# A transformer block on one core: the first output projection's weights asked for together, divisions at 18 exponentials instead of 28, and block 0's statistics four exponentials later

## The chip, the core and the metric

The kernel runs on one core of a Trainium2 chip. The metric is the device time of one execution in microseconds (us). Engines are named as in the profile: PE (TensorE, matrix products), DVE (VectorE), ACT (ScalarE), POOL (GpSimd), SP (SyncE, which here issues the DMAs). Each engine works through its own instructions in the order in which they were written; semaphores tie the engines together.

## The reference

One transformer block with an adaptive layer norm, for 2048 rows of 512 features, 32 heads of 16, and a feed-forward layer of 1792. Everything is fp32.

```python
def _A_ref(x, wqkv, wo):                       # attention
    qkv = (x @ wqkv).reshape(B, S, 3, H, Dh).transpose(2, 0, 3, 1, 4)
    q, k, v = qkv[0], qkv[1], qkv[2]
    scores = einsum("bhqd,bhkd->bhqk", q, k) * Dh ** -0.5
    o = einsum("bhqk,bhkd->bhqd", softmax(scores), v)
    return o.transpose(0, 2, 1, 3).reshape(B, S, D) @ wo
def _B_ref(x, w1, b1, w2, b2):                 # feed-forward
    return einsum("bsf,fd->bsd", gelu(einsum("bsd,df->bsf", x, w1) + b1), w2) + b2
sa, ca, ga, sb, cb, gb = six rows of silu(c) @ w_mod
x = x + ga * _A_ref(layernorm(x) * (1 + ca) + sa, ...)
x = x + gb * _B_ref(layernorm(x) * (1 + cb) + sb, ...)
```

## The kernel before

**Tiles.** Where the result needs nearly full fp32, a value is kept as two pieces, a high and a low one, and a product is three matmuls (high × high, low × high, high × low). A weight tile that holds both pieces of 128 rows of `wo`, `w1` or `w2` has 512 KB. The rows are cut into four blocks of 512 queries.

**Stages.** A prologue, whose order is a list written out by hand, does the layer norm and the first projections. Then come 512 half-steps. They belong to 32 units (query block × group of four heads) of 16 half-steps each, and a half-step handles 128 keys. It has four score matmuls for the exponentials (L642, ACT's exponential at L649), four score matmuls ahead of that for the row maxima of a later unit (L390, DVE's reduction at L395), and the products of the probabilities with the values of an earlier half-step (`pv`, L676). Everything else of the block, that is the other projections, the output projection and the feed-forward layer, is background: groups of matmuls that add up in one bank named `bg`. A half-step takes six half-row matmuls of the current group along (L276). A half-step for which no group is ready is called empty here; it writes its fourth maximum's scores to the free `bg` bank, which is how the profile tells it apart. In the last 22 half-steps no maxima are left, and a half-step takes four half-row matmuls of background. What is still open after the 512th half-step is done in a tail without scores.

**What sets the order.** The Python program writes the instructions in the order in which they shall stand. Its clock `t` counts exponentials (in the tail every second matmul). `later(n, f)` writes the step `f` when n more exponentials have been written, and `soon(n, f)` does so too but also counts the step as owed until then. `work()` yields the background groups one after another and yields nothing where a condition isn't met; that makes a half-step empty. So a delay in the code is a place in the order, and what the engines do with it shows only in the trace.

**The steps that the change touches**, in the order in which they come:
- `proj_qk` (L300 and on): a projection group's end. ACT copies the bank (L310), POOL makes the two pieces (L311, L312), and a `soon` step stores them to memory (`store_qk`, L298 and L299, 768 KB in two DMAs on SP).
- `block0` waits until nothing is owed and no division is under way, then calls `open_ffn` (L684 and on), which gives up the pools of the projections and opens one pool for the output projection and the feed-forward layer in the same memory. A tile of the new pool waits for the last user of its memory.
- `wload` (L776 to L792) asks for the next weight tile in the order of use, at SP's line L791, if fewer than WB = 8 tiles are taken. Half-steps call it, at most once each.
- `o_prep` (L708 to L748), the softmax division for one quarter of a block's features: it asks for the denominators `dn` and the sums `ob`; then DVE's reciprocal (L724), a store of it (L728), a load spread over rows, `rb` (L734), and on POOL the product and its two pieces (L742 to L744). Each step comes a number of exponentials after the one before it: 14, 2, 5 and 7, which makes 28.
- `front(b)` (L812 and on), the output projection of a block: it waits for four divisions and four exponentials more, until all four `wo` tiles have been asked for, and then yields four groups of four half-steps each. Behind a group stand ACT's copy (L859), the addition of `x` on POOL (L862), and after a number of exponentials the statistics: two parts on DVE (L839), four exponentials apart, the aggregate and the factor (L842, L851, and L852 on POOL), then the normalization `xn` on POOL (L825). Block 0's last group takes a shorter way, on DVE.
- At a unit's end its maxima are brought together on DVE (L407, L409), split in two on POOL (L411, L412, tile `m`), stored (L416) and loaded into the rows of `qst` (L422). SP also asks for the keys (`kh`, L362), the values (`vg`, L595), `x` (L810), and stores the attention's sums (`ou`, L665).

Of the kernel before, what the change touches and what calls it, by code (L numbers as in the profile page):

```python
# [23 lines left out]
KC = D // P  # L24
NB = 4
# [45 lines left out]
def block_kernel(ctx: ExitStack, tc: tile.TileContext, x, wqkv, wo, w1, b1, w2, b2, c, w_mod, out):  # L71
# [4 lines left out]
    def pool(name, bufs=1, **kw):  # L76
        cm = tc.tile_pool(name=name, bufs=bufs, **kw)
        return cm, cm.__enter__()

    def close(*cms):  # L80
        for cm in cms:
            cm.__exit__(None, None, None)
# [78 lines left out]
    def stage(name):  # L161
        if first[0] and name in FIRST:
            return vpool.tile([P, D], F32, tag=name, name=name, bufs=FIRST[name])
        return spool.tile([P, D], F32, tag=name, name=name, bufs=STAGE[name])

    def pieces(name, dt=FR):
        return spool.tile([P, 2, D], dt, tag="parts", name=name, bufs=3)
# [83 lines left out]
    def later(n, f):  # L251
        if n:
            hooks.setdefault(clock["t"] + n, []).append(f)
        else:
            f()
# [3 lines left out]
    def soon(n, f):  # L259

        owed[0] += 1

        def g():
            owed[0] -= 1
            f()

        later(n, g)
# [27 lines left out]
    def store_qk(w, k, b, parts):  # L295
        stored.add((w, k, b))
        planes = qk_d[w][k].rearrange("i d o t -> (d o) i t")[:, :, b * TB : (b + 1) * TB]
        sy.dma_start(planes[:, 1 - w : 3 - w], parts.bitcast(F32))  # L298
        sy.dma_start(planes[:, 2 * w], parts[:, 0].bitcast(F32))  # L299

    def proj_terms(w, k, b):
        hi, lo = hT[b]
        t = wt_of[w, k]
        n = range(KC)
        return terms3([t[:, 0, i] for i in n], [t[:, 1, i] for i in n], [hi[:, i] for i in n], [lo[:, i] for i in n])

    def proj_qk(w, k, b):
        def evac(ps):
            parts, r = pieces("parts"), stage("pf")
            ac.activation(r, ps, AF.Copy)  # L310
            gp.tensor_copy(parts[:, 0], r)  # L311
            gp.tensor_tensor(parts[:, 1], r, parts[:, 0].bitcast(F32), op=ALU.subtract)  # L312
            soon(8, lambda: store_qk(w, k, b, parts))

        return proj_terms(w, k, b), "bg", evac

# [372 lines left out]
    def open_ffn():  # L689
        assert not preps and not owed[0]  # L690
        close(*pools["old"])
        pools["cm"], pools["f"] = pool("ffn", side="right")
        f = pools["f"]
        pools["x2"] = [[f.tile([P, D], F32, name=f"x2{n}{i}") for i in range(4)] for n in range(2)]

    pcs = []

# [6 lines left out]
    def tmp(name):  # L704
        if "f" in pools:
            return pools["f"].tile([P, D], F32, tag="t", name=name, bufs=8)
        return dvpool.tile([P, D], F32, tag="t", name=name, bufs=4)

    free_pc, busy, over = [0], [0], [False]

    def o_prep(b, k):

        dn = small.tile([P, 32], F32, tag="dn", name="dn")
        base = ou_d[b]
        sy.dma_start(dn, base[2 * k : 2 * k + 2].rearrange("g (j r) (a f) -> (g j) r a f", r=32, f=32)[:, DH])
        ob, rb = tmp("ob"), tmp("rb")
        for g in range(2):
            sy.dma_start(ob[g * 64 : (g + 1) * 64], base[2 * k + g].rearrange("(j r) t -> j r t", r=32)[:, :DH])
        eng = ve if over[0] else gp
        r = rden_d[b][k * 8 : (k + 1) * 8]  # L720
        busy[0] += 1

        def inv():
            ve.reciprocal(dn, dn)  # L724
            later(0 if over[0] else 2, store)

        def store():
            sy.dma_start(r.rearrange("h (a f) -> (h a) f", f=32), dn)  # L728
            later(1 if over[0] else 5, load)
            if over[0]:  # L730
                wload()

        def load():
            sy.dma_start(rb, bass.AP(tensor=r.tensor, offset=r.offset, ap=[[TB, 8], [0, DH], [1, TB]]))  # L734
            later(9 if over[0] else 7, div)
            if over[0]:
                for _ in range(6):
                    wload()
                load_x2(last, x2)

        def div():
            eng.tensor_tensor(ob, ob, rb, op=ALU.mult)  # L742
            eng.tensor_copy(pc(b, k, 0), ob)
            eng.tensor_tensor(pc(b, k, 1), ob, pc(b, k, 0).bitcast(F32), op=ALU.subtract)  # L744
            done[b] += 1
            busy[0] -= 1

        later(11 if over[0] else 14, inv)  # L748

    def try_prep():  # L750
        if not ready or not pcs:
# [26 lines left out]
    def wload():  # L778

        n = len(wt)  # L780
        if n == len(stream) or "f" not in pools:
            return
        key = stream[n]
        if extra:
            t = extra.pop()
        elif len(ringed) < WB or ringed[-WB] in used:
            t = pools["f"].tile([P, 2, D], FR, tag="w", name=f"w{key[1]}", bufs=WB)
            ringed.append(key)
        else:
            return  # L790
        sy.dma_start(t.bitcast(F32), {"o": wo_d, 1: w1_d, 2: w2_d}[key[1]][key[2]])  # L791
        wt[key] = t  # L792
# [14 lines left out]
    def load_x2(b, x2):  # L807
        for t in range(4):
            r0 = b * TB + t * P
            sy.dma_start(x2[t], x[r0 : r0 + P, :])  # L810

    def front(b, x2):  # L812


        later(9, lambda: load_x2(b, x2))
        yield from until(lambda: done[b] == KC - 1)
        yield from wait(4)
        yield from loaded(b, *[("o", k) for k in range(KC)])
        mv = small.tile([P, 4, 2], F32, tag="mv", name="mv")
        rs = {}  # L820
        xn = {}

        def norm(t):
            xn[t] = tmp("xn")
            (gp if b or t < 3 else ve).tensor_scalar(  # L825
                xn[t], x2[t], mv[:, t, 0:1], rs[t], op0=ALU.subtract, op1=ALU.mult)
            later(40, lambda: gp.tensor_tensor(x2[t], x2[t], b2_b, op=ALU.add))
            if b and len(xn) == 4:
                later(9, lambda: sides.extend([lambda fc=fc: trans(fc, "mx") for fc in range(KC)]))

        def stat(t):
            if b == 0 and t == 3:
                ln_stat(mv, t, x2[t])
                later(1, lambda: factor(t))
                return
            st = small.tile([P, 2, 6], F32, tag="bsh", name="bsh")

            def part(i):
                ve.bn_stats(st[:, i], x2[t][:, i * HD : (i + 1) * HD])  # L839

            def whole():
                ve.bn_aggr(mv[:, t], st)  # L842
                factor(t)

            part(0)
            later(4, lambda: part(1))
            later(8, whole)

        def factor(t):
            rs[t] = small.tile([P, 1], F32, tag=f"rt{t}", name=f"rt{t}")  # L850
            ve.tensor_scalar(rs[t], mv[:, t, 1:2], EPS, None, op0=ALU.add)  # L851
            gp.tensor_tensor(rs[t], rs[t], mhalf[:, 0:1], op=ALU.pow)  # L852
            later(3 if t < 3 else 2, lambda: norm(t))

        for t in range(4):

            def evac(ps, t=t):
                y = tmp("y")
                ac.activation(y, ps, AF.Copy)  # L859

                def add():
                    gp.tensor_tensor(x2[t], y, x2[t], op=ALU.add)  # L862
                    later(8 if b else 4 if t < 3 else 3, lambda: stat(t))

                later(2, add)

            yield o_terms(b, t, range(KC)), "bg", evac
        drop(b, *[("o", k) for k in range(KC)])
        t0 = clock["t"]

        def trans(fc, bk="bg"):
            ps = take(bk)
            for t in range(4):
                te.transpose(ps[:, t * P : (t + 1) * P], xn[t][:, fc * P : (fc + 1) * P], ident)  # L874
            h = tmp("h32")
            ac.activation(h, ps, AF.Identity, scale=modc[:, 1, fc, 0:1], bias=modc[:, 1, fc, 1:2])
            gp.tensor_copy(pc(b, fc, 0), h)
            gp.tensor_tensor(pc(b, fc, 1), h, pc(b, fc, 0).bitcast(F32), op=ALU.subtract)
            turned[fc] = clock["t"]

        turned = {}
        yield "ln"
        if b:
            yield from until(lambda: len(turned) == KC and clock["t"] >= turned[KC - 1] + 8)
            return
        yield from until(lambda: len(xn) == 4 and clock["t"] >= t0 + 9)
        for fc in range(KC):
            yield lambda fc=fc: trans(fc)
        yield from wait(4)
# [410 lines left out]
```

## Time and profile before

| | |
|---|---|
| median of 3 runs | 1693.07 us (1692.38 to 1693.36) |
| the profiled execution | 1691.76 us |
| its span, first to last instruction | 1690.0 us |
| granted TensorE clock, mean | 0.997 |
| background of the half-steps: `wo`, `w`×`g`, `pchi`×`w` matmuls | 192, 1056, 656 |
| half-step exponentials | 2048, 611 ns each |

The table of groups in the profile gives line, engine, operation, output tile and input tiles, shape and count, then the busy time and the mean time of one in ns. The timeline gives start, duration, engine, line, operation and, in brackets, the idle time just before and what ended it. `SPq` is the DMA queue of SP: the duration of its rows is the issue, not the transfer.

### The profile page before, as it was taken

Reading aid. Unit: us, or ns where it says so; the run is one execution under the profiler, and the core shown is the slowest. Engines: PE = TensorE matmul, PEld = TensorE weight load, DVE = VectorE, ACT = ScalarE, POOL = GpSimd, SP = SyncE. Lnnn points to the kernel's source line nnn. Section 1 sums busy time; section 2 is a strip of 40 time slices with the busy share of each in tenths; the row PEclk is TensorE's granted clock in tenths of the full one; section 3 lists DMA queues with packets and bytes.
Section 4 is the critical chain, followed back from the end, with each engine's and each line's share of the span. In section 5 each row is a group of like instructions: output and inputs, shape, how many; then the busy total and the mean of one; then the engine's idle time right before and its main releaser. Section 6 shows DMA issues by size and latency. Waiting matters only on the chain.

```text
span 1690.0 us, 32259 instructions
## 1 busy us (share of the span) xinstructions
PE 1670.4 (99%) x12121; PEld 919.3 (54%) x12121; DVE 1402.7 (83%) x2692; ACT 1238.0 (73%) x2379; POOL 692.0 (41%) x698
## 2 busy tenths in 40 slices
PE   7999999999999999999999999999999999999999
PEld 6655555555554455555555555555555555553777
DVE  8998888889889988898999888888999888880332
ACT  3358788788777788778877788778877788779131
POOL 7323443434211356405643447316633456226110
PEclk8999999999999999999999999999999999999999
DMA  9656666657557434326454454345453454333544
GB/s 297 204 175 189 219 208 208 219 185 229 145 152 220 118 90 119 90 47 175 118 161 106 114 164 121 84 117 140 115 164 79 131 145 107 84 96 109 208 153 157
DMA packets 137127, 251.88 MB, mean 149 GB/s; under 512 B 25854, under 2 KB 45324, under 8 KB 136972
## 3 DMA queue, kind: packets, MB, share of 16 engines
q1 hardware_dynamic: 135712, 248.19, 50.6%
q8 instruction: 96, 1.57, 0.4%
q10 hardware_dynamic: 1260, 1.63, 0.3%
q14 instruction: 59, 0.48, 0.1%
HBM read 188.49 MB, written 61.28 MB: 148 GB/s over the span
## 4 chain that ended last, share of the span: by engine, by line
PE 91%; DVE 4%; DMA 2%; ACT 2%; issue 0%; POOL 0%; SPq 0%; POOLq 0%; ACTq 0%; DVEq 0%
PE bg L276 40%; PE pv L676 29%; PE e L642 16%; PE mx L390 4%; DVE mxp L395 3%; ACT p L649 1%; DMA kh<-qk 1%; PE pr L276 1%; PE o L276 1%; PE warm L441 1%; PE mx L335 0%; DVE bst L237 0%; DMA qst<-qk 0%; PE mx L874 0%; DMA qk<-parts 0%; DMA wraw<-in_A_wqkv_dram 0%
## 5 line engine op out<-in xcount | busy, mean ns | idle before, releaser
L395 DVE TENSOR_REDUCE mxp<-mx 128x1 f32<-128x512 f32 x2034 | 1285.0, 682 | 143.3 <-PE mx L390 126.3
L649 ACT ACTIVATE p<-e 128x512 f32<-128x512 f32 x2048 | 1073.0, 611 | 272.5 <-PE mx L390 251.3
L390 PE MATMUL mx<-kh,qst 48*128 48x512 f32 x2034 | 835.6, 423 | 1.3 <-DVE mxp L395 1.0
L642 PE MATMUL e<-qst,kh 50*128 50x512 f32 x2048 | 777.9, 424 | 3.7 <-ACT p L649 3.6
L642 PEld LDWEIGHTS e<-qst,kh 50*128 50x128 f32 x2048 | 341.4, 185 | 429.6 <-ACT p L649 309.8
L676 PE MATMUL pv<-p,vg 128*32 128x512 f32 x4096 | 546.3, 605 | 0.3 <-ACT osb L663 0.3
L390 PEld LDWEIGHTS mx<-kh,qst 48*128 48x128 f32 x2034 | 367.0, 185 | 14.9 <-DVE mxp L395 9.7
L276 PE MATMUL bg<-w,g 64*128 64x512 f32 (+1 forms) x1056 | 264.3, 389 | 0.1
L276 PEld LDWEIGHTS bg<-w,g 64*128 64x128 f32 (+1 forms) x1056 | 196.0, 186 | 29.7 <-issue 0.5
L276 PE MATMUL bg<-pchi,w 64*128 64x512 f32 (+1 forms) x656 | 177.8, 391 | 0.0
L676 PEld LDWEIGHTS pv<-p,vg 128*32 128x32 f32 x4096 | 81.0, 108 | 171.7 <-issue 159.0
L276 PE MATMUL bg<-hThi,wqkv 64*128 64x512 f32 x560 | 153.1, 392 | 0.1
L276 PEld LDWEIGHTS bg<-pchi,w 64*128 64x128 f32 (+1 forms) x656 | 120.8, 185 | 25.6 <-DVE tick L1086 5.9
L276 PEld LDWEIGHTS bg<-hThi,wqkv 64*128 64x128 f32 x560 | 103.8, 185 | 14.1 <-DVE tick L1108 0.4
L918 POOL TENSOR_SCALAR s<-s 128x512 f32<-128x512 f32 x40 | 59.9, 1497 | 97.0 <-ACT s L916 96.6
L937 POOL TENSOR_TENSOR x<-y,x 128x512 f32<-128x512 f32 x28 | 36.0, 1285 | 153.0 <-ACT y L936 153.0
L276 PE MATMUL bg<-pclo,w 64*128 64x512 f32 (+1 forms) x328 | 88.5, 389 | 0.0
L276 PE MATMUL bg<-hTlo,wqkv 64*128 64x512 f32 x280 | 76.5, 392 | 0.0
L911 POOL TENSOR_TENSOR s<-h 128x512 f32<-128x512 f32 x40 | 41.7, 1042 | 69.2 <-ACT h L910 69.2
L276 PEld LDWEIGHTS bg<-pclo,w 64*128 64x128 f32 (+1 forms) x328 | 60.0, 184 | 13.1 <-DVE tick L1086 5.0
L276 PE MATMUL bg<-wo,pchi 64*128 64x512 f32 x192 | 59.3, 388 | 0.0
L411 POOL CAST m<-mt 128x32 fp32r<-128x32 f32 x32 | 6.8, 212 | 121.7 <-DVE mt L409 121.7
(165 smaller groups left out, 1373.8 us busy)
## 6 DMA issues: line engine op xcount, KB each, us to landing
kh<-qk SPq DMA_DIRECT2D x256, 192.0 KB
w<-w1s SPq DMA_DIRECT2D x56, 512.0 KB
w<-w2s SPq DMA_DIRECT2D x54, 512.0 KB
vg<-v SPq DMA_DIRECT2D x64, 332.0 KB
qk<-parts SPq DMA_DIRECT2D x32, 512.0 KB
qst<-qk SPq DMA_DIRECT2D x64, 192.0 KB
qk<-parts SPq DMA_DIRECT2D x32, 256.0 KB
ou<-osb SPq DMA_DIRECT2D x32, 256.0 KB
```

The costliest lines, as they stand in the source:

```text
L276: return te.matmul(ps, term[0][r], term[1][r], start=i == 0, stop=i == n - 1)
L390: te.matmul(ps, qst[u][r0 : r0 + KR, p, qc * P : (qc + 1) * P], kh(u, kr // 2)[r0 : r0 + KR, p, (kr % 2) * TB : (kr % 2 + 1) * TB], start= ...
L395: ins = ve.tensor_reduce(mxp[u][:, hc, kr : kr + 1], ps, axis=AX.X, op=ALU.max, negate=True)
L411: gp.tensor_copy(m2[:, 0], mt)
L441: te.matmul(warm[:, :P], ident, ident, start=True, stop=True)
L642: ins = te.matmul(ps, kh(u, kc // 8)[r0 : r0 + KX, p, (kc % 8) * P : (kc % 8 + 1) * P], qst[u][r0 : r0 + KX, p], start=True, stop=True)
L649: op = ac.activation(t, ps, AF.Exp, scale=SCALE)
L676: te.matmul(cur["ps"][32 * j : 32 * (j + 1)], vg[u][:, kc, j * VW : j * VW + 32], pt.pop(4 * s + j), start=kc == 0, stop=kc == NKC - 1)
L911: gp.tensor_tensor(s, h, h, op=ALU.mult)
L918: gp.tensor_scalar(s, s, 1.0, None, op0=ALU.add)
L937: later(4, lambda: gp.tensor_tensor(x2[t], y, x2[t], op=ALU.add))
```

## The change

- The store of the very last projected piece is written two exponentials after its group's end, not eight.
- `open_ffn` asks for the first four weight tiles (the four of `wo`) at once, when the new pool opens. Before, the half-steps asked for one each.
- The delays of a division in the half-steps become 10, 1, 3 and 4 exponentials, 18 together; those of the tail stay.
- Block 0's statistics for its first three row tiles follow the addition by eight exponentials, not four, as in the other blocks.

```diff
-            soon(8, lambda: store_qk(w, k, b, parts))
+            soon(2 if (w, k, b) == (0, KC - 1, NB - 1) else 8, lambda: store_qk(w, k, b, parts))
...
         pools["x2"] = [[f.tile([P, D], F32, name=f"x2{n}{i}") for i in range(4)] for n in range(2)]
+        for k in range(KC):
+            wload()
...
         def inv():
             ve.reciprocal(dn, dn)
-            later(0 if over[0] else 2, store)
+            later(0 if over[0] else 1, store)
...
             sy.dma_start(r.rearrange("h (a f) -> (h a) f", f=32), dn)
-            later(1 if over[0] else 5, load)
+            later(1 if over[0] else 3, load)
...
-            later(9 if over[0] else 7, div)
+            later(9 if over[0] else 4, div)
...
-        later(11 if over[0] else 14, inv)
+        later(11 if over[0] else 10, inv)
...
                     gp.tensor_tensor(x2[t], y, x2[t], op=ALU.add)
-                    later(8 if b else 4 if t < 3 else 3, lambda: stat(t))
+                    later(8 if b or t < 3 else 3, lambda: stat(t))
```

Behind the two new lines in `open_ffn`, line numbers of the changed kernel are two higher.

What moves in the order shows at three places. The first is SP around the opening of the new pool, between the last projection and the first output projection; `qk_86<-parts` are the two DMAs of the last projection's store, `wos_132` to `wos_135` the four `wo` tiles in memory, `kh_191` the keys of a unit, `in_A_x_dram` the input `x`, `m` the rows of maxima. Before:

```order
L416 DMA m_101<-m_7417 4x32x32 x2
L422 DMA qst<-m_101 2x1024 x2
L298 DMA qk_86<-parts 128x2x512
L299 DMA qk_86<-parts 128x512
L362 DMA kh_191<-qk_88 48x2x512 x2
L791 DMA wo<-wos_132 128x1024
L791 DMA wo<-wos_133 128x1024
L362 DMA kh_191<-qk_88 48x2x512 x2
L810 DMA x_7589<-in_A_x_dram 128x512
```

And in the changed kernel:

```order
L416 DMA m_101<-m_7420 4x32x32 x2
L298 DMA qk_86<-parts 128x2x512
L299 DMA qk_86<-parts 128x512
L422 DMA qst<-m_101 2x1024 x2
L793 DMA wo<-wos_132 128x1024
L793 DMA wo<-wos_133 128x1024
L793 DMA wo<-wos_134 128x1024
L793 DMA wo<-wos_135 128x1024
L362 DMA kh_191<-qk_88 48x2x512 x2
L793 DMA w_7648<-w1s_136 128x1024
```

The store stands ahead of the load of the maxima's rows, all four `wo` requests stand together, and the loads of `kh_191` and `x` stand behind them. On PE the first `bg<-wo` matmul moves four half-steps ahead, to the third half-step after the last projection's; the program leaves 12 half-steps empty instead of 14.

The second place is POOL at the first output projection; `x_7589` and `x_7590` (`x_7557` and `x_7558` in the changed kernel) are the first two row tiles of block 0, `rt` the factor of the first. Before:

```order
L862 TENSOR_TENSOR x_7589<-y,x_7589 128x512
L852 TENSOR_TENSOR rt_8051<-rt_8051,mhalf 128x1
L411 CAST m_8085<-mt 128x32
L412 TENSOR_TENSOR m_8085<-mt,m_8085 128x32
L825 TENSOR_SCALAR xn<-x_7589,mv,rt_8051 128x512
L862 TENSOR_TENSOR x_7590<-y,x_7590 128x512
```

And in the changed kernel:

```order
L864 TENSOR_TENSOR x_7557<-y,x_7557 128x512
L854 TENSOR_TENSOR rt_7961<-rt_7961,mhalf 128x1
L864 TENSOR_TENSOR x_7558<-y,x_7558 128x512
L827 TENSOR_SCALAR xn<-x_7557,mv,rt_7961 128x512
L411 CAST m_8121<-mt 128x32
L412 TENSOR_TENSOR m_8121<-mt,m_8121 128x32
```

The second addition now stands ahead of the first normalization and of the split of the maxima.

The third place is PE from the last `pv` matmuls of the half-steps on, where the tail begins; `bg<-pchi` and `bg<-pclo` are groups of the feed-forward layer's first product, `bg<-w,g` of its second. Before:

```order
L676 MATMUL pv<-p,vg 32x512 x8
L276 MATMUL bg<-pchi_5392,w_22733 128x512 x8
L276 MATMUL bg<-pclo_5393,w_22733 128x512 x4
L276 MATMUL bg<-pchi_5392,w_22821 128x512 x8
L276 MATMUL bg<-pclo_5393,w_22821 128x512 x4
L276 MATMUL bg<-w_22881,g 128x512 x3
```

And in the changed kernel:

```order
L676 MATMUL pv<-p,vg 32x512 x8
L276 MATMUL bg<-pchi_5392,w_22755 128x512 x8
L276 MATMUL bg<-pclo_5393,w_22755 128x512 x4
L276 MATMUL bg<-w_22843,g 128x512 x3
L276 MATMUL bg<-w_22895,g 128x512 x3
L276 MATMUL bg<-w_22951,g 128x512 x3
```

One group of 12 matmuls has left the tail. The last four half-steps, which had no background before, hold some of it.

## The prediction

> **What bounds the kernel now.** I read the page first: busy times, then the chain that ended last.
>
> ```profile
> span 1690.0 us, 32259 instructions
> PE 1670.4 (99%) x12121; PEld 919.3 (54%) x12121; DVE 1402.7 (83%) x2692; ACT 1238.0 (73%) x2379; POOL 692.0 (41%) x698
> PE 91%; DVE 4%; DMA 2%; ACT 2%; issue 0%; POOL 0%; SPq 0%; POOLq 0%; ACTq 0%; DVEq 0%
> ```
>
> TensorE (PE) is busy for 99% of the span and carries 91% of the chain. So an edit pays only if it takes matmuls away, keeps PE from standing still, or puts matmuls into time in which PE would stand. The last kind of time exists: half-steps without a background group. They can be counted, because there the fourth maximum's matmul is written to the `bg` bank:
>
> ```profile
> L390 PE MATMUL bg<-kh,qst 48*128 48x512 f32 x14 | 5.6, 399 | 0.4 <-DVE mxp L395 0.4
> ```
>
> There are 14. Six lie ahead of the first output projection, where the change works; the PE timeline shows two of them, the first `wo` matmul, and the fourth (which needs the second weight tile):
>
> ```profile
> 516.05 1.06 PE L676 MATMUL pv<-p,vg 128*32 128x512 f32 x8
> 518.67 1.06 PE L676 MATMUL pv<-p,vg 128*32 128x512 f32 x8
> ...
> 529.21 1.07 PE L676 MATMUL pv<-p,vg 128*32 128x512 f32 x8
> 530.54 0.39 PE L276 MATMUL bg<-wo,pchi 64*128 64x512 f32 x1
> ...
> 531.24 0.39 PE L276 MATMUL bg<-wo,pchi 64*128 64x512 f32 x1
> ...
> 532.05 1.07 PE L676 MATMUL pv<-p,vg 128*32 128x512 f32 x8
> ```
>
> From `pv` to `pv` an empty half-step takes 2.62 us, a filled one 2.84; the first `wo` matmul stands 1.33 us behind its `pv`, the fourth 0.70 later. A group moved into an empty half-step thus saves a filled half-step elsewhere and costs only 0.22 here.
>
> **The change, part by part.** The profiled execution took 1691.76 us (1690.0 of span and 1.76 around it); the median of the runs is 1693.07. I make the sum against the former and shift both alike.
>
> *1. The first `wo` matmul moves to the third half-step after the last projection, four earlier.* It then stands 1.33 us behind the `pv` at 518.67: PE gets there at 520.0. Nothing ahead of it is slower than before, and PE works in order: scores, exponentials and `pv` behind it wait too. Are the weights there? They go into memory that the last projection's pieces leave, so their request waits for the store of these pieces. SyncE's timeline, and its waits between 480 and 560 us:
>
> ```profile
> 516.20 0.39 SPq L298 DMA_DIRECT2D qk<-parts  x1
> 516.64 0.46 SPq L299 DMA_DIRECT2D qk<-parts  x1
> 517.19 1.45 SPq L362 DMA_DIRECT2D kh<-qk  x2
> 520.92 0.81 SPq L791 DMA_DIRECT2D wo<-wos  x2
> ...
> 524.63 0.43 SPq L791 DMA_DIRECT2D wo<-wos  x1
> ```
> ```profile
> SPq L791 <- DMA qk<-parts: 2.2, 1, 2.2
> ```
>
> The first request waited 2.2 us for the store and went out at 520.92, after PE's new arrival. `soon(2)` doesn't help: the store was issued as soon as GpSimd had made the pieces, not on the count. What helps is that the two `kh` loads now stand behind the weights. DMA rates from 516 us on, in slices of 0.4 us:
>
> ```profile
> GB/s 0 0 97 369 384 399 369 261 251 338 200 184 62 36 82 82 164 297 461 399 420 399 364 323 154 205 241 220 133 189 277 389 394 384 384 420 399 420 379 379
> ```
>
> By 519.2 these slices sum to 0.75 MB, the store's 768 KB: without the loads it ends between 519.3 and 520.9. I take the middle, 520.1. The first tile's landing: the third request stands behind the same semaphore as the first and went out at 524.63, so the first took at most 3.7 us; data begins at about 522.4, 1.5 us after the issue, and 512 KB at 400 GB/s takes 1.3, so at least 2.8. I take 3.5, near the semaphore's bound. The first tile is there at 523.6 to 523.7, the stall 3.7 us. Then 0.70 us of matmuls to the second tile, which lands 1.3 after the first on a full queue: another 0.6 to 0.7. Together **+4.4** (ends: 519.3 + 2.8 + 0.6 − 520.0 = 2.7; 520.9 + 3.7 + 0.6 − 520.0 = 5.2, and 5.9 if the second tile shares the queue as it did before). Tiles three and four are needed two half-steps later, 5.7 us: nothing. The rows of maxima (`qst<-m`) now stand behind the store on SP and go out after 517.1; the unit that uses them begins two half-steps behind 518.67, at 523.9, and waits with PE: nothing either.
>
> [...]
>
> *2. The clock behind the stall.* In the prologue PE also stood still. Windows of 3.41 us: PE busy, PEld, DVE, ACT, POOL, then the granted clock:
>
> ```profile
> 12.91:16.33 3.42, 2.70 (x23) 1.67 (x22) 0.97 (x2) 0.60 (x1) 1.56 (x1) 1.00 1.08 364
> 16.33:19.74 3.41, 2.78 (x23) 2.18 (x21) 2.22 (x7) 1.76 (x3) 2.56 (x3) 1.00 1.09 356
> 19.74:23.16 3.42, 2.03 (x9) 1.33 (x10) 3.31 (x8) 3.10 (x6) 3.34 (x4) 1.00 1.04 386
> 23.16:26.57 3.41, 3.37 (x9) 2.13 (x8) 3.38 (x5) 0.01 (x1) 3.24 (x5) 0.50 1.05 387
> ...
> 29.98:33.40 3.42, 1.43 (x12) 0.96 (x9) 3.35 (x8) 2.54 (x4) 3.15 (x6) 1.00 0.67 249
> 33.40:36.81 3.41, 3.00 (x12) 2.26 (x12) 3.41 (x4) 2.56 (x5) 2.85 (x4) 0.50 0.61 221
> ```
>
> After PE was busy 2.70 of 3.42 (79%) the clock stayed; after 2.03 (59%) and 1.43 (42%) the next window ran at 0.50. A stall of 3.7 us cuts some window under 59% wherever the windows fall. A half-clock window in which PE works throughout does 1.7 us less; as part of it can fall on the second stall and on the half-step's time that PE does not set (2.62 against 2.84 shows that another engine is close), I take **+1.1**, with 0.5 and 1.75 as ends.
>
> [...]
>
> *3. Empty half-steps.* The planner now leaves 12 empty, not 14: 2 × 0.22 = **+0.4**. This is what the work at the end gains from.
>
> *4. Block 0's statistics, four exps later.* VectorE stood here, and PE with it:
>
> ```profile
> 553.14 0.22 DVE L407 TENSOR_REDUCE mn<-mxp 128x16 f32<-128x64 f32 x1
> 553.39 0.21 DVE L409 STREAM_TRANSPOSE mt<-mn 128x32 f32<-128x32 f32 x1
> 554.21 2.08 POOL L825 TENSOR_SCALAR xn<-x,mv,rt 128x512 f32<-128x512 f32 x1
> 554.74 1.06 PE L676 MATMUL pv<-p,vg 128*32 128x512 f32 x8
> 556.26 1.29 POOL L862 TENSOR_TENSOR x<-y,x 128x512 f32<-128x512 f32 x1
> 557.59 0.43 DVE L839 BATCH_NORM_STATS2 bsh<-x 128x6 f32<-128x256 f32 x1 [1.55 <-POOL x L862]
> 559.09 1.07 PE L676 MATMUL pv<-p,vg 128*32 128x512 f32 x8
> ```
>
> The add of `x` is queued on GpSimd behind a 2.08-us normalization, the statistic waits 1.55 us for it, the reductions behind it wait too, and the half-step takes 4.35 us instead of 2.84: 1.5 lost. Four exps are one half-step, 2.8 us, more than 1.55, and the add is now queued ahead of the normalization: **−1.5**. In return the statistic's end meets the unit's end (L407, L409: 0.43 us) in one half-step: 0 to +0.43, taken as **+0.3**.
>
> *5. Divisions at 18 exps.* An exp is 2.84 / 4 = 0.71 us. The reciprocal comes 10 exps = 7.1 us after its data was asked for; the slowest landing above took 4.3 (516.64 to 520.9). The division comes 4 exps = 2.8 us after `rb` is asked for, so GpSimd may wait a us or two on it, with additions and casts behind it; at 41% busy it catches up. If it didn't, a statistic would meet a late add as in 4, for 1.5. Cost **0**.
>
> *6. The last half-steps.* The background is two half-steps ahead at the end, so the last four, empty before, now hold matmuls:
>
> ```profile
> 1554.13 1.06 PE L676 MATMUL pv<-p,vg 128*32 128x512 f32 x8
> ...
> 1556.25 1.07 PE L676 MATMUL pv<-p,vg 128*32 128x512 f32 x8
> ...
> 1564.03 2.90 PE L676 MATMUL pv<-p,vg 128*32 128x512 f32 x16
> ```
> ```profile
> 1562.53 3.31 ACT L649 ACTIVATE p<-e 128x512 f32<-128x512 f32 x6
> ```
>
> The four took 1564.03 − 1556.25 = 7.78 us; four filled ones at 2.12 take 8.5: at most +0.7. But ScalarE's 16 exponentials at 3.31 / 6 = 0.55 take 8.8 and run to the end either way. I take **+0.2**.
>
> *7. The tail.* One feed-forward group of 12 matmuls is gone from it:
>
> ```profile
> 1566.87 2.11 PE L276 MATMUL bg<-pchi,w 128*128 128x512 f32 x8
> 1568.82 1.08 PE L276 MATMUL bg<-pclo,w 128*128 128x512 f32 x4
> 1569.74 1.98 PE L276 MATMUL bg<-pchi,w 128*128 128x512 f32 x8
> ```
> ```profile
> 1586.46 11.07 PE L276 MATMUL o<-wt,kh 128*128 128x512 f32 x48
> ```
> ```profile
> 1577.17 2.08 SPq L791 DMA_DIRECT2D wt<-wos  x4
> ```
>
> 1569.74 − 1566.87 = −2.87. What is late next is the last projection's weights, asked for at 1577.17 in either kernel: PE now wants them at 1583.6. PE uses a tile in 3 × 11.07 / 48 = 0.7 us and the queue brings one in 1.3, so the three tiles behind the first could cost up to 3 × 0.6 = 1.8; I take +1.1. Net **−1.8** (ends −2.9 and −1.0).
>
> **Sum:** 4.4 + 1.1 + 0.4 − 1.5 + 0.3 + 0 + 0.2 − 1.8 = +3.1: 1694.9 profiled, a median of **1696.2** (+0.18%). A measurement of this kernel tells about 0.2% from no change, which is 3.4 us.
>
> **The rivals.**
> - *A, the forecast (0.53):* a stall of about 4.4 and one half-clock window; +1.6 to +4.6 by the ends of the terms. Just under 3.4 lies a little more of it than above: 0.31 within, 0.22 slower.
> - *B, slower (0.20):* the store's end doesn't gain from the loads' move and stays at 520.9, tiles one and two land as they did, and the stall of 5.9 lies across a window border, so that two windows drop. 5.9 + 1.75 in place of 4.4 + 1.1 gives +5.2: 1698.3. For it: the 2.2-us wait is a measured one. It decides from a store's end of about 520.4 on.
> - *C, little change (0.15):* the clock stays up, by the row at 12.91 a matter of how the windows cut the stall, or the stall is near its lower end. Sum +1.4 (no clock term and 0.6 less stall): 1694.5.
> - *D, no stall (0.12):* PE arrives later than I have it, or the memory is free earlier, and the weights are in time. Then 4.4 and 1.1 go: −2.4, down to −3.9 if the tail gives its whole 2.9 and the end costs nothing: 1690.7 (0.07 faster, 0.05 within). Against it: 520.92 is after 520.0.
>
> **How the numbers follow.** Faster 0.07 (from D); within 0.2%: 0.31 + 0.15 + 0.05 = 0.51; slower 0.22 + 0.20 = 0.42. The range from 1693.0 to 1699.0 takes in A, C and most of B and leaves out D and B's upper end.
>
> **What would show it.** In the changed kernel: PE's first `bg<-wo,pchi` near 523.7 with idle time before it put down to the DMA of `wo`; one window of 0.50 clock right behind; 12 rows in place of 14 in the group of empty half-steps; no VectorE wait for `x` near 550; one group of 12 ahead of the tail's long row, and idle time ahead of the second or third `wo` tile there. It would be wrong if the first `wo` matmul finds its weights (D), if the store's end stays at 520.9 (B), or if GpSimd's earlier divisions delay an add that PE then waits for.

## The result, and the profile after

The changed kernel is slower: a median of 1705.80 us in six runs (1701.87 to 1708.63) against 1693.21 us (1692.38 to 1693.95), a ratio of 1.0073 (95% interval 1.0062 to 1.0084). Forecast were 1696.2 us and a range up to 1699.0. The profiled execution took 1701.87 us, the fastest of the six; so what follows accounts for 10.1 us of a typical difference of 12.6.

The page of the changed kernel; PE is still busy for almost all of the time, 3 us longer than before in a span that is 10 us longer:

```profile
span 1700.0 us, 32299 instructions
PE 1673.3 (98%) x12133; PEld 921.1 (54%) x12133; DVE 1404.2 (83%) x2696; ACT 1238.6 (73%) x2379; POOL 700.0 (41%) x705
```

If the starts of `pv` in the two timelines are subtracted half-step by half-step, the difference falls into few places. In the prologue it is −0.5 us. In the two half-steps from 404.3 us on it is +4.8, in the two from 523.1 us on +7.2, at the statistics −1.5; all other half-steps, in steps of under 1 us both ways, make +1.8, and the tail, counted from its first matmul, −1.9. Together +9.9, and the spans differ by 10.0.

**At the first output projection** the stall is the one that was forecast. PE's timeline, then SyncE's, in the changed kernel:

```profile
523.08 1.07 PE L676 MATMUL pv<-p,vg 128*32 128x512 f32 x8
528.33 0.76 PE L276 MATMUL bg<-wo,pchi 64*128 64x512 f32 x1 [3.75 <-issue]
529.74 0.62 PE L276 MATMUL bg<-wo,pchi 64*128 64x512 f32 x1
531.18 1.93 PE L676 MATMUL pv<-p,vg 128*32 128x512 f32 x8
```
```profile
521.05 0.46 SPq L299 DMA_DIRECT2D qk<-parts  x1
524.49 1.76 SPq L793 DMA_DIRECT2D wo<-wos  x4
```

The weights' requests go out 3.44 us behind the last store, whose end they wait for (SyncE's waits between 515 and 530 us put 1.4 us, in two, down to it), and the first `wo` matmul starts 3.84 us behind them; PE stood idle for 3.75 us. The profile says "issue" there, not the DMA; that it is the weights is read from the order of the program and from the run below that moves the group. Ahead of the fourth matmul there is no idle time: the second tile was in time. But the matmuls last 0.62 us instead of 0.39, and so the fourth comes 1.41 us behind the first instead of 0.70; whether the tile would have been in time at full speed isn't shown. Windows of 3.41 us, laid where the clock switches (PE, PEld, DVE, ACT, POOL busy, granted clock, DMA share, GB/s):

```profile
524.33:527.75 3.42, 0.24 (x2) 0.00 (x0) 0.88 (x2) 0.60 (x1) 0.00 (x0) 1.00 0.61 189
527.75:531.16 3.41, 2.83 (x12) 1.90 (x12) 1.38 (x2) 1.49 (x3) 0.00 (x0) 0.50 1.00 404
531.16:534.57 3.41, 3.41 (x18) 1.43 (x18) 1.42 (x3) 0.99 (x3) 0.00 (x0) 0.50 1.06 243
534.57:537.99 3.42, 3.42 (x30) 1.98 (x28) 2.85 (x7) 2.38 (x5) 0.00 (x0) 1.00 1.04 387
```

Two whole windows run at half clock, not one.

**Near 405 us** there is a loss that the forecast did not have. VectorE in the changed kernel, and PE:

```profile
404.88 0.68 DVE L395 TENSOR_REDUCE mxp<-mx 128x1 f32<-128x512 f32 x1
409.23 0.35 DVE L726 RECIPROCAL dn<-dn 128x32 f32<-128x32 f32 x1 [3.67 <-DMA dn<-ou]
```
```profile
410.18 0.49 PE L390 MATMUL mx<-kh,qst 48*128 48x512 f32 x1 [3.00 <-DVE mxp L395]
```

A division's reciprocal waits 3.67 us for its denominators, the row maxima's reductions are queued behind it, no bank for maxima comes free, and PE stands 3.00 us. A window of halved clock follows here too:

```profile
408.32:411.73 3.41, 1.55 (x11) 0.47 (x13) 2.50 (x6) 0.00 (x0) 1.04 (x1) 1.00 0.99 264
411.73:415.15 3.42, 3.42 (x18) 2.19 (x22) 2.53 (x5) 1.86 (x4) 0.00 (x0) 0.50 0.86 292
```

Why the denominators were late stands on SyncE. `rden` is the store of a division's reciprocals, `rb` the load that reads it back, `ou` the store of a unit's attention sums, `dn` the request for the next division's denominators, which are read from `ou`. Before:

```profile
393.49 0.58 SPq L728 DMA_DIRECT2D rden<-dn  x1
394.17 0.38 SPq L665 DMA_DIRECT2D ou<-osb  x1
...
398.28 0.59 SPq L734 DMA_DIRECT2D rb<-rden  x1
...
399.47 0.60 SPq L715 DMA_DIRECT2D dn<-ou  x1
```

And in the changed kernel:

```profile
393.95 0.38 SPq L730 DMA_DIRECT2D rden<-dn  x1
399.90 0.59 SPq L736 DMA_DIRECT2D rb<-rden  x1
400.55 0.45 SPq L665 DMA_DIRECT2D ou<-osb  x1
...
404.70 0.59 SPq L717 DMA_DIRECT2D dn<-ou  x1
```

Counted from its division's request, the load now stands 14 exponentials behind (10, 1 and 3) instead of 21, and `rb` has passed `ou` in SyncE's order. `rb` waits for `rden` to land, `ou` now stands behind it and goes out 6.4 us later, and `dn` waits for `ou`. SyncE's waits between 390 and 405 us name both, the first with up to 5.5 us at a time (before it was 1.4), the second with 0.2:

```profile
SPq L736 <- DMA rden<-dn: 8.0, 2, 5.5
...
SPq L717 <- DMA ou<-osb: 0.2, 1, 0.2
```

The reciprocal, which the change puts four exponentials earlier, is there first. In the kernel before it came with room to spare:

```profile
408.89 0.34 DVE L724 RECIPROCAL dn<-dn 128x32 f32<-128x32 f32 x1
```

**The gains** came as forecast, but for the last half-steps. Twelve half-steps are empty; the statistic no longer waits for its addition, and its half-step takes 561.23 − 558.38 = 2.85 us instead of 4.35; the tail begins with one group:

```profile
L390 PE MATMUL bg<-kh,qst 48*128 48x512 f32 x12 | 4.8, 401 | 0.8 <-DVE mxp L395 0.8
```
```profile
558.38 1.07 PE L676 MATMUL pv<-p,vg 128*32 128x512 f32 x8
559.57 0.42 DVE L841 BATCH_NORM_STATS2 bsh<-x 128x6 f32<-128x256 f32 x1
561.23 1.07 PE L676 MATMUL pv<-p,vg 128*32 128x512 f32 x8
```
```profile
1578.74 2.11 PE L276 MATMUL bg<-pchi,w 128*128 128x512 f32 x8
1580.69 1.08 PE L276 MATMUL bg<-pclo,w 128*128 128x512 f32 x4
1581.61 12.40 PE L276 MATMUL bg<-w,g 128*128 128x512 f32 x54
...
1596.41 0.96 PE L276 MATMUL o<-wt,kh 128*128 128x512 f32 x3 [0.31 <-DMA wt<-wos]
1597.70 2.56 PE L276 MATMUL o<-wt,kh 128*128 128x512 f32 x10 [0.32 <-DMA wt<-wos]
```

The four half-steps that were empty at the end and now hold matmuls take 1576.13 − 1567.59 = 8.54 us, where the kernel before took 7.78. (In the table of the kernel before, the 1056 and 656 matmuls hold 240 and 16 of the tail; its half-steps have 816 and 640.)

```profile
1567.59 1.07 PE L676 MATMUL pv<-p,vg 128*32 128x512 f32 x8
...
1576.13 2.67 PE L676 MATMUL pv<-p,vg 128*32 128x512 f32 x16
```

### The profile page after: what moved, and what is told of

The parts are those of the page before. It is cut to its first block, busy times and chain, and to the rows that moved or that the text cites. A ratio compares the mean times of both kernels' runs of the same rounds, so it can differ in the third digit from the quotient of the medians.

```text
span 1700.0 us, 32299 instructions
## 1 busy us (share of the span) xinstructions
PE 1673.3 (98%) x12133; PEld 921.1 (54%) x12133; DVE 1404.2 (83%) x2696; ACT 1238.6 (73%) x2379; POOL 700.0 (41%) x705
## 4 chain that ended last, share of the span: by engine, by line
PE 92%; DVE 4%; DMA 2%; ACT 1%; issue 0%; SPq 0%; POOL 0%; ACTq 0%; DVEq 0%
PE bg L276 40%; PE pv L676 30%; PE e L642 16%; PE mx L390 4%; DVE mxp L395 2%; PE pr L276 1%; PE o L276 1%; DMA wm<-in_w_mod_dram 0%; PE mx L335 0%; DMA wt<-wos 0%; DMA w<-w2s 0%; ACT p L649 0%; DVE bst L237 0%; DMA qst<-qk 0%; PE mx L876 0%
## 5 line engine op out<-in xcount | busy, mean ns | idle before, releaser
L276 PEld LDWEIGHTS bg<-hTlo,wqkv 64*128 64x128 f32 x280 | 52.2, 187 | 7.6
```

The lines of the kernel that those rows point to most:

```text
L276: return te.matmul(ps, term[0][r], term[1][r], start=i == 0, stop=i == n - 1)
```

## The experiments

The theory after these traces: the loss has two places, each a matter of order. (1) The load `rb` passed `ou` on SyncE; (2) the first output projection stands two half-steps too early for its weights. Rivals: 18 exponentials are too few wherever the load stands; the divisions are harmless and the excess is scatter; four requests at once are slow. "The kernel before" is run beside each; its medians in these sessions were 1692.77, 1693.59 and 1692.91 us.

**Old delays in the changed kernel**

```diff
-later(0 if over[0] else 1, store) ... 3, load) ... 4, div) ... 10, inv)
+later(0 if over[0] else 2, store) ... 5, load) ... 7, div) ... 14, inv)
```

> The changed kernel with the four delays of a division back at 14, 2, 5 and 7. Theory (late denominators): the changed kernel loses about 4.8 us in the two half-steps near 405 us, where the reciprocal waits 3.7 us for its denominators and the row maxima queue behind it on VectorE. With the old delays this wait is gone, the 6.8 us at the first output projection stay (two half-steps of 8.10 and 4.37 us), the second group of 12 matmuls is back in the tail. Time 1693.2 + 6.8 - 1.5 + 0.4 = 1698.9, and the runs lie within 1.5 us of each other. Rival (the divisions are harmless, the rest and the scatter of the changed kernel come from its first output projection): 1705.8 + 1.9 for the group in the tail, about 1707.

Measured: 1700.56 us, ratio 1.0043 (1.0028 to 1.0058). The wait near 405 us is gone; the two half-steps at the first output projection take 8.05 and 3.80 us. That is 5.2 us under the changed kernel although 12 matmuls are back in the tail. The rival is out. The runs lie within 3.0 us of each other, not 1.5 as expected. The 1.7 us over the expected time can be due to the clock: the profiled run's mean granted clock is 0.992, where the changed kernel's first profile has 0.995, and it has a halved window at 582 us, shown at the end, that the other has not.

**Only the new delays in the kernel before**

```diff
-later(0 if over[0] else 2, store) ... 5, load) ... 7, div) ... 14, inv)
+later(0 if over[0] else 1, store) ... 3, load) ... 4, div) ... 10, inv)
```

> The kernel before with only the divisions' delays changed, 10, 1, 3 and 4. The order of background groups and the empty half-steps stay as they were. Theory (late denominators): one wait of VectorE for the denominators of 3 to 5 us near 405 us and a stretch of halved clock behind it, 1693.2 + 5 to 7 = 1698 to 1700, with more scatter than before. Rival (harmless): 1693.2, within 0.5.

Measured: 1699.22 us, ratio 1.0041 (1.0026 to 1.0056). The waits of VectorE show the same wait, and the loss is 6.4 us by the medians:

```profile
DVE dn L724 <- DMA dn<-ou: 3.5, 1, 3.5
```

So the divisions alone make a loss of this size, without the weights' move. In the profile 4.6 us of it lie in the same two half-steps and 1.7 near 424 us, where ScalarE waits for a block of the projections' weights (`wraw`); its request, at 410.52 us before, now stands behind the next `rb`, at 421.36. The waits between 420 and 431 us:

```profile
ACT wqkv L192 <- DMA wraw<-in_A_wqkv_dram: 1.6, 1, 1.6
```

**Only the reciprocal's delay back, in the changed kernel**

```diff
-        later(11 if over[0] else 10, inv)
+        later(11 if over[0] else 14, inv)
```

> The changed kernel with only the reciprocal's delay back at 14 (14, 1, 3, 4: 22 together). The program still has 12 empty half-steps and one group fewer in the tail. Theory (it is the reciprocal, written 2.85 us earlier, that meets late denominators): VectorE's wait near 405 us falls from 3.7 to under 0.9 us and no clock is lost there; 1705.8 - 4.8 or more, 1697 to 1700. Finer rival (the early load of the spread rows holds SyncE, and so the next division's request is late whatever the reciprocal's delay): a wait of over 2 us stays, 1701 or more.

Measured: 1700.27 us, ratio 1.0047 (1.0032 to 1.0062). The wait near 405 us is gone, as expected, but the time is just above the expected 1697 to 1700: in the last half-steps, from 1524.7 us on, two take 4.39 and 3.18 us instead of 3.00 and 2.30, with a window of halved clock (3.41 us) from 1530.6 on. The waits between 1522 and 1537 us:

```profile
POOL ob L744 <- PE mx L390: 2.5, 1, 2.5
...
ACT s L918 <- POOL s L915: 2.0, 1, 2.0
```

GpSimd stands 2.5 us before a division, ScalarE's tanh 2.0 us for GpSimd, with the exponentials behind it. PE had been done by then; that it was `rb`, asked for only four exponentials earlier, is argued and not tested. The division before it speaks for `rb`: there the profile names `rb`, and the division starts 4.28 us after `rb` was asked for (1511.00 to 1515.28); here it is 4.22 (1516.87 to 1521.09). This kernel does not tell which delay matters either, because its store and load also stand four exponentials later, and `ou` is ahead of `rb` again.

**Only the reciprocal's delay at ten, in the kernel before**

```diff
-        later(11 if over[0] else 14, inv)
+        later(11 if over[0] else 10, inv)
```

> The kernel before with only the reciprocal's delay at 10 (10, 2, 5, 7: 24 together). The reciprocal stands 2.85 us earlier behind its request. If the nearness alone makes the stall, a wait of over 1 us shows and the time is 1695 or more. If it takes the early load on SyncE as well (5.2 us later request in the changed kernel than in the one before), no wait of VectorE for denominators over 0.5 us shows and the time is 1693.2, within 0.5.

Measured: 1693.79 us, ratio 1.0007 (0.9998 to 1.0017), and no wait for denominators in the profile. The median is 0.6 us over the 1693.2 expected, where 0.5 was given, and 1.0 over the kernel before beside it; the runs don't tell this from none. The nearness of the reciprocal alone does not make the loss of 6.4 us.

**18 exponentials with the load behind `ou`**, in the kernel before

```diff
-later(0 if over[0] else 2, store) ... 5, load) ... 7, div) ... 14, inv)
+later(0 if over[0] else 1, store) ... 6, load) ... 1, div) ... 10, inv)
```

> The kernel before with the divisions at 10, 1, 6, 1: 18 together and the reciprocal at 10, as in the changed kernel, but the load of the spread rows stands 17 exponentials behind the request, not 14, so that on SyncE the store of the attention's sums near 395 us (ou, L665) stands ahead of it again. Theory (the load crossed that store: it holds SyncE until the row before it is stored, the sums go out 5 to 6 us late, and the denominators, which are read from the sums, with them): no wait of VectorE for denominators over 0.5 us near 405 us; 1693 to 1695. Rival (18 exponentials are too few, whatever stands where): the wait of about 3.5 us and the loss of 6.4 us that the kernel with 10, 1, 3 and 4 had stay, about 1699.

Measured: 1693.96 us, ratio 1.0000 (0.9990 to 1.0009). SyncE's order is that of before, and the reciprocal finds its data:

```profile
395.23 0.77 SPq L728 DMA_DIRECT2D rden<-dn  x1
396.09 0.41 SPq L665 DMA_DIRECT2D ou<-osb  x1
400.48 0.59 SPq L734 DMA_DIRECT2D rb<-rden  x1
402.14 0.99 SPq L715 DMA_DIRECT2D dn<-ou  x1
```
```profile
408.70 0.34 DVE L724 RECIPROCAL dn<-dn 128x32 f32<-128x32 f32 x1
```

This is the run that decides. Reciprocal at 10 and 18 in all, as in the run that lost 6.4 us; only the load stands three exponentials later (and the division, in its old place, one behind it instead of four), and the loss is gone.

**The last projection's store back at eight exponentials**, in the changed kernel

```diff
-            soon(2 if (w, k, b) == (0, KC - 1, NB - 1) else 8, lambda: store_qk(w, k, b, parts))
+            soon(8, lambda: store_qk(w, k, b, parts))
```

> The changed kernel with the store of the last projected piece back at eight exponentials. The pool then opens later, the four weight requests are still written together, and the first output projection stands two half-steps later, in the third half-step after 518 us in place of the first; 12 half-steps are empty and the tail has one group less, as in the changed kernel. Theory (PE came 3.9 us too early for the first weights; two half-steps are 5.2 us): no idle time of PE ahead of the first wo matmul, no halved clock behind it, both half-steps at 2.6 to 2.9 us; 1705.8 - 6.8 = 1699, the loss near 405 us stays. Rival (four requests at once are slow, so that PE waits wherever the group stands): a wait of over 1 us stays, 1702 or more.

Measured: 1697.83 us, ratio 1.0023 (1.0013 to 1.0032), 8.0 us under the changed kernel's median. SyncE asks for the four tiles at 526.31 us and PE comes to them at 531.40, without idle time and at full clock:

```profile
526.31 1.76 SPq L793 DMA_DIRECT2D wo<-wos  x4
```
```profile
530.07 1.06 PE L676 MATMUL pv<-p,vg 128*32 128x512 f32 x8
531.40 0.39 PE L276 MATMUL bg<-wo,pchi 64*128 64x512 f32 x1
...
532.08 0.39 PE L276 MATMUL bg<-wo,pchi 64*128 64x512 f32 x1
...
532.90 1.07 PE L676 MATMUL pv<-p,vg 128*32 128x512 f32 x8
```

So four requests at once are not slow; it was two half-steps too early. The loss near 405 us is still there, and here it has a second part: the half-step from 405.25 us on takes 2.3 us more than in the kernel before, and the two from 421.84 on take 3.5 more, with ScalarE's wait of 2.0 us for `wraw` and a halved window (3.41 us) from 426.2 on. Again the request for `wraw`, at 419.62, stands behind an `rb` that went out at 418.97.

**Only the statistics**, in the kernel before

```diff
-                    later(8 if b else 4 if t < 3 else 3, lambda: stat(t))
+                    later(8 if b or t < 3 else 3, lambda: stat(t))
```

> The kernel before with only block 0's statistics at eight exponentials. Theory: VectorE's wait of 1.55 us for the addition near 556 us is gone, the half-step of 4.35 us takes 2.84, and the unit's end costs some 0.2 to 0.3 us more elsewhere: 1.2 to 1.5 us less than before. Rival (the time comes back within a few half-steps, since the statistic is late for the normalization): no difference.

Measured: 1692.10 us against 1693.59, ratio 0.9993 (0.9984 to 1.0002): by the runs not told from none. In the trace the half-step of 4.35 us takes 558.19 − 555.35 = 2.84, and no later half-step is longer than before by more than 0.4 us:

```profile
555.35 1.06 PE L676 MATMUL pv<-p,vg 128*32 128x512 f32 x8
558.19 1.06 PE L676 MATMUL pv<-p,vg 128*32 128x512 f32 x8
```

**Both places mended, short divisions only where a front waits**

```diff
-            later(0 if over[0] else 1, store)
+            later(0 if over[0] else 1 if b in (1, 2) and k == 3 else 2, store)
...
-        later(11 if over[0] else 10, inv)
+        later(11 if over[0] else 10 if b in (1, 2) and k == 3 else 14, inv)
...
-        yield from wait(4)
+        yield from wait(4 if b else 8)
```

> The changed kernel with the short divisions kept only for the last quarter of blocks 1 and 2, where a block's front waits for them, and with block 0's front waiting four exponentials longer, which puts its first group two half-steps later. 12 empty half-steps and one tail group less, as in the changed kernel. Theory (both losses of the changed kernel, near 405 and near 520 us, are due to these places alone): both are gone, the gain of the statistic and of the tail stays: 1692.8 - 1.5 + 0.2 + 0.5 - 1.9 = 1690.1, 0.16% less than before. Rival (the short divisions of blocks 1 and 2 cost as well): 1693 or more.

Measured: 1692.44 us against 1693.59, ratio 0.9990 (0.9981 to 0.9999). The profile shows neither loss and one tail group. The gain is 1.2 us where 2.7 were expected, and its interval ends just under 1.

**Both places mended, all divisions at 18 exponentials**

```diff
-later(1 if over[0] else 3, load) ... 4, div)
+later(1 if over[0] else 6, load) ... 1, div)
-        yield from wait(4)
+        yield from wait(4 if b else 8)
```

> The changed kernel with all divisions still at 18 exponentials, but as 10, 1, 6, 1 (the load behind the store of the sums again), and block 0's front four exponentials later. Theory (not the 18 exponentials and not the four requests at once cost time, but these two placements): no wait for denominators near 405 us, none for the first weights; 1693.6 - 1.5 - 1.9 + 0.7 = 1691 to 1692.5, as the kernel with three short divisions. Rival (a division one exponential behind its load makes GpSimd wait 3 to 4 us in each of sixteen divisions, and statistics and tanh behind it): 1695 or more.

Measured: 1691.62 us against 1692.91, ratio 0.9995 (0.9986 to 1.0004). Everything that the change set out to do is in this kernel but for two placements, and it is not slower than before; that it is faster, the interval doesn't show. The rival, GpSimd's waits, is out.

**The changed kernel again**

> The changed kernel again, unaltered, since its profiled execution (1701.87 us) was the fastest of its six and 3.9 us under their median. Theory (the excess of a typical run is more of the same: longer waits near 405 and 420 us, whose length depends on when DMAs land there, and whole windows of halved clock of 3.4 us, 1.7 us lost for each): in a profile nearer the median the half-steps outside 400 to 430 and 520 to 540 us take as long as in the kernel before to within 0.5 us, and those two places take 2 to 5 us more than in the first profile. Rival: the excess lies in the prologue (which differed by up to 2.7 us between the profiles so far) or is spread over the span.

Measured: 1704.69 us, ratio 1.0069 (1.0053 to 1.0084); the profiled run took 1704.73, 2.9 us more than the first profile. My theory holds only in part: 2.0 us of the 2.9 lie in the prologue, where the rival had it. Near 405 us the halved clock lasts two windows this time, and the second of the two half-steps takes 0.9 us more, but the first takes 0.3 less:

```profile
407.33:410.74 3.41, 1.70 (x13) 1.06 (x11) 0.30 (x2) 2.06 (x4) 3.25 (x4) 1.00 1.03 347
410.74:414.16 3.42, 2.71 (x11) 0.61 (x11) 2.51 (x6) 0.00 (x0) 0.44 (x1) 0.50 1.00 232
414.16:417.57 3.41, 3.41 (x18) 2.21 (x22) 2.19 (x4) 1.77 (x4) 0.00 (x0) 0.50 0.79 259
```

Where the slowest run of 1708.63 us spent its time stays open. Its mean granted clock was 0.992 where the first profile's was 0.995, so halved windows can be a part of it; but a run of 1705.78 us had 0.995 as well.

## Why the prediction was wrong

The step that failed is number 5, "Divisions at 18 exps", costed at **0**. It counted 10 exponentials, 7.1 us, from the request for the denominators and set the slowest landing in view, 4.3 us, against it. Both numbers were near (here the denominators took 4.5 us, from 404.70 to 409.23), but the count starts where the request is written, and SyncE reached it late: the load of the division before it, moved ahead of `ou`, held the queue for 5.5 us, and the request waits for `ou`. The step asked which data each moved instruction waits for, and not what is queued behind a moved instruction that waits. The order on SyncE around `rb` was the place to look at; the forecast follows SyncE only around the weights. Measured price: 4.8 us in the changed kernel's first profile, 6.4 by the medians alone. Without it the result would have lain about at the upper end of the range, 1699.0: the run with the old divisions took 1700.56 us, of which 1.9 are the tail group that it keeps.

Step 1 was right in mechanism and near in size: the store ended 3.44 us after its issue where 520.1 − 516.64 = 3.46 was taken, the first tile came 3.84 us after its request instead of 3.5, and the stall was 3.75 us. The further 0.7 for the second tile did not come, and the fourth matmul, at half clock, came later too. Step 2 was mis-sized: +1.1 for one halved window with part of it hidden; it was two windows, 6.83 us at half clock, some 3 us. Together the two were given 5.5; the two half-steps lost 7.2, of which 0.44 is that they are filled. That the sum came near is in part luck, since 0.65 too much in step 1 stood against some 2 too little in step 2. Rival B had the two windows, for another reason (a stall across a border). Here PE was busy for 0.24 us of the first window, and behind the next, with 2.83 us of 3.41 busy, the clock stayed halved.

Steps 3, 4 and 7 held: 12 empty half-steps; −1.5 at the statistics, and its collision with the unit's end adds 567.13 − 564.07 − 2.84 = 0.2; −1.9 in the tail against −1.8, with less waiting for the last weights (0.31 and 0.32 us at two tiles) than the 1.1 taken. Step 6 did not: it took +0.2, on the ground that ScalarE's exponentials set the end either way, and the four half-steps took 8.54 − 7.78 = 0.76 more, its upper end; they lasted as long as four filled ones, 4 × 2.12 = 8.5.

Two sums of the forecast do not come out. The lower end of rival D is −2.4 − 1.1 − 0.2 = −3.7, not −3.9. And the ends given for the terms reach from about −0.8 to +6.0 when they are added up, wider than the +1.6 to +4.6 of rival A; the measured +10.1 lies outside either.

With step 5 at its measured 4.8 and steps 1 and 2 together at 6.8 in place of 5.5, the sum would have been 3.1 + 4.8 + 1.3 = +9.2, and with step 6 at its 0.76 +9.8; the profiled execution shows +10.1. The direction of the forecast was right, the size a quarter of what was measured.

## What to carry to other kernels

When a step is moved, read the whole order of its queue around both its old and its new place: an instruction that waits, moved up, costs its wait to whatever it has passed, and to all who wait for that (here 5.5 us of SyncE's queue). Count a margin from when a request leaves its queue, not from where it is written. And where PE is the bound, look at the granted clock behind a stall as well as at the stall: in the changed kernel's first profile the stalls of 3.00 and 3.75 us were followed by 3.41 and 6.83 us at 0.50 clock, by an estimate (half of that time) up to 1.7 and 3.4 us more.

## What the runs showed of the hardware

The granted clock of the two main profiles reads 1.00 or 0.50, and a stretch at 0.50 lasted 3.41 us or 6.83, but for the one that runs into the end of the span (from 1688.86 us on before, from 1698.53 in the changed kernel). Before there are three others, from 23.16, 33.40 and 40.22 us on; in the changed kernel's first profile four, from 22.59, 36.24, 411.73 and 527.75 us on. They start at no fixed place of the program: in the changed kernel's second profile the stretch near 405 us starts 1.0 us earlier than in the first (410.74 against 411.73), the one at the first output projection 2.4 us later (530.2 against 527.75).

How long PE was busy in a window of 3.41 us at full clock, and the granted clock of the window behind it:

| profile | window from (us) | PE busy (us) | clock behind |
|---|---|---|---|
| before | 12.91, 16.33, 555.63 | 2.70, 2.78, 2.37 | 1.00 |
| before | 19.74, 29.98, 36.81 | 2.03, 1.43, 1.39 | 0.50 |
| changed kernel, first | 29.41, 404.91, 582.37 | 1.82, 2.27, 2.60 | 1.00 |
| changed kernel, first | 19.17, 32.83, 408.32, 524.33 | 1.94, 1.76, 1.55, 0.24 | 0.50 |
| changed kernel, second | 407.33 | 1.70 | 0.50 |
| old delays in the changed kernel | 578.56 | 2.61 | 0.50 |
| both places mended, all at 18 | 577.90 | 2.60 | 0.50 |

So the forecast's bound of 59% was not a sharp one: 1.82 us, 53% of a window, were followed by full clock, and 2.60 us, 76%, once by full clock and once by half. The way back was no sharper in PE's busy time. Halved windows with 2.83 (527.75 us, changed kernel) and 2.71 us (410.74 us, its second profile) were followed by another; those with 3.00 to 3.42 us in the first profiles of both kernels (3.37, 3.00 and 3.27 before, 3.06, 3.01, 3.42 and, from 531.16 on, 3.41 in the changed one) by full clock; and one with 3.41 us, from 581.32 on in the kernel with both places mended and all divisions at 18, by another halved one. The window from 578.56 on, at the empty half-steps near 580 us, in the kernel with the old divisions:

```profile
578.56:581.97 3.41, 2.61 (x20) 1.12 (x16) 3.41 (x6) 2.31 (x5) 1.27 (x2) 1.00 0.00 0
581.97:585.39 3.42, 3.42 (x16) 1.10 (x9) 2.71 (x5) 1.76 (x5) 0.00 (x0) 0.50 0.08 29
```

At the same place in the one with both places mended and all divisions at 18, two half-steps took 8.95 us against 6.29 in the other kernel with both places mended. By its length and its clock a halved window of 3.41 us costs up to 1.7 us (an estimate, 0.50 × 3.41), and the clock bears out that it makes a part of the scatter between runs of one kernel: of the 60 runs of the kernel before beside the experiments (1690.65 to 1695.26 us), the five with a mean granted clock of 0.999 took 1691.4 us on average, the five with 0.995 took 1694.3. It isn't all of it: the 19 runs with 0.998 alone spread from 1691.09 to 1694.58, and the prologue, which no edit touches, took 111.4 us to its first `pv` before, with three halved windows, and 110.9 in the changed kernel's first profile, with two: 0.5 us apart, where one window can cost 1.7. That is why differences of 1 to 2 us had to be read from half-steps and not from medians.
